# Sparse attention and a feed-forward block on one core: token blocks of 512 instead of 256, with the split done in place and the weights converted without GpSimd

## The chip, the cores and the metric

The kernel runs on one core of a Trainium2 chip. The metric is the device time of one execution in microseconds (us). The kernel before took 999.59 us, the median of three runs (999.54 to 1001.24).

Engines go by the profile's names: PE is TensorE's products and PEld its weight loads, DVE is VectorE, ACT ScalarE, POOL GpSimd, SP SyncE. An engine works through its own list of instructions in order; the engines meet at semaphores. DMA transfers are issued from the lists of SP and ACT.

## What is computed

Eight batches, eight heads, 576 positions, head size 64. Heads 0 to 3 attend within 32 positions back (local), heads 4 to 7 to earlier positions of the same class modulo 32 (strided). The result, 576 x 512 per batch, goes through a low-rank mix over the positions and a feed-forward layer:

```
scores = scale * q @ k.T                              # masked, then softmax
x      = softmax(scores) @ v                          # all heads side by side: (8, 576, 512)
u      = x + ((x.T @ U) @ V).T                        # U: 576 x 32, V: 32 x 576
out    = u + relu(u @ w_ch1) @ w_ch2                  # w_ch1: 512 x 2048, w_ch2: 2048 x 512
```

U, V and both weights arrive as 64-bit floats; q, k and v are 32-bit. For the large products each operand is split into a high and a low part (`uh`, `ul`; `gh`, `gl`; two parts of each weight chunk), and three products (high-high, high-low, low-high) are summed.

## The kernel before, in words

**Feed-forward part.** Tokens are cut into tiles of 128. A batch has four tiles of its own and half a tile more; the halves of two batches share the tile `xt`. Two tiles make a block of 256 tokens, so there are 18 blocks. A block runs 16 steps, one per chunk of 128 hidden units. `gemm1` (L546) makes 12 products of 256 columns into `ph`; ScalarE's relu makes `gh` (L550), VectorE `gl` (L551). `gemm2` (L562) makes six products of 512 columns per step into `acc`, two steps behind `gemm1`. `finish` (L569) adds `acc` to `u` and stores it.

**Ahead of a block.** `transposes` brings `u` into columns by token. For the first three blocks TensorE does it (L512) and ScalarE and VectorE split the result (L516, L517). For the others VectorE transposes 32 x 32 pieces (`bt`, L525), 16 transfers on SP move them into `u`, and L534 and L535 split them into new buffers `uh`, `ul`, five buffers of tag `u` in turn.

**Weights.** `weights` turns 64-bit words into 32-bit floats with one ScalarE instruction (L115) and three of VectorE (L117, L118, L120), in halves of 512 columns; ScalarE casts the high part (L162), GpSimd subtracts for the low part (L163). Sixteen chunks of 1 MB are loaded, three at first (`AHEAD`) and then each after the GpSimd copy L144 that waits for a converted chunk. Four chunks are converted ahead of the first product (`PRE`), and the first two blocks run interleaved (`NLEAD`, `SKEW`) while the rest are converted.

**Attention.** Two heads make a pair. A pair has mask and scores (L234, L240), softmax (L249, L250, L254), transposes (L261, L264), outputs (L273) and a normalisation (L283 to L285). Batches 0 and 1 do all heads so; their two strided pairs are computed in class order, and their outputs `od` go through DRAM to come back in token order into `xg`. Batches 2 to 7 do the local pairs so, and the strided heads on GpSimd and VectorE: products on GpSimd (L327, L355), each summed by a VectorE reduction (L329, L357), the result copied into `xg` by ScalarE (L372, L376). `mix_t` (L393, L397) makes `x.T @ U` as four products side by side in the array, whose parts are added (L402, L404) and split into `tst` (L407 to L409); `mix_u` (L419, L421, L427, L428) adds the correction to `x`.

**What sets the order.** A loop over the steps interleaves `gemm1`, `gemm2`, conversion and attention by windows of steps (`W0`, `W1`, `N_LOCAL`, `CONVM`). A scheduler then reorders each engine's instructions by its own estimate of the times. PSUM holds one `acc` of two banks, two `ph` and two `px` of two banks each; attention and mixing use `px`, and `acc` too until the first product.

Of the kernel before, what the change touches and what calls it, by code (L numbers as in the profile page):

```python
# [16 lines left out]
ATT_BUFS = 4  # L17
NSP = 2
N_STEPS_1 = 90
N_LOCAL = 48  # L20
# [3 lines left out]
W0, W1 = 2, 29  # L24
N_PE_T = 3
AHEAD = 3
PRE = 4
CONVM = 1.35
NLEAD = 2
SKEW = 2  # L30
CLA = 2
S_END = 16
# [5 lines left out]
def fused_kernel(ctx, tc, pairs, strided, U, V, w_in, masks, eye, out):  # L38
# [7 lines left out]
    NDC = DM // 128  # L46

# [33 lines left out]
    def psx2():  # L81

        banks["n"] += 1
        if banks["prefix"] and banks["n"] % 3 == 0:
            return ps_acc.tile([128, 2, 512], F32, name="acc")
        return ps_x.tile([128, 2, 512], F32, name="px")
# [8 lines left out]

    def od_dma(out, in_):
        nc.scalar.dma_start(out=out, in_=in_)
# [3 lines left out]
    mask_s = ubuf([128, 320], "mask_s", BF16)  # L101
    mask_l, ident_b = masks_sb[:, 0:320], masks_sb[:, 320:448]
    U_sb = const.tile([128, 5, R], F32, name="U_sb")
    Vst = const.tile([96, S], F32R, name="Vst")
    raws, w_parts = {}, {}
# [32 lines left out]

    def load_weights():
        for fc in range(NFC):  # L140
            raw = raws[fc] = const.tile([128, 1024], I64, name=f"w{fc}", tag=f"w{fc}")
            if fc >= AHEAD:
                done = w_parts[fc - AHEAD].bitcast(F32)
                nc.gpsimd.tensor_copy(out=raw.bitcast(F32)[:, 0:1], in_=done[:, 1, 1, 0:1])  # L144
            nc.sync.dma_start(out=raw, in_=w_in[128 * fc:128 * fc + 128, :])
            yield

    def weights():
        for fc in range(NFC):
            load_ahead(fc + 1)  # L150
            fs = []
            for i in range(2):
                early = i and fc < NFC - AHEAD - 2
                cv = late_part[fc % 2][:, 1536:2048] if early else ap_.tile([128, 512], F32, name="cv", tag="cv", bufs=2)
                behind = [marks[k][2] for k in ("less", "exp")] if fc < PRE else marks["split0"]
                with tc.issue_after(behind[0]), tc.issue_after(behind[1]):
                    fs.append(to_f32(raws[fc][:, 512 * i:512 * i + 512], cv, 128, 512))
                if not i:
                    yield
            parts = w_parts[fc] = const.tile([128, 2, 2, 512], F32R, name=f"w{fc}", tag=f"w{fc}")  # L160
            for i in range(2):
                nc.scalar.copy(out=parts[:, i, 0], in_=fs[i])  # L162
                nc.gpsimd.tensor_tensor(out=parts[:, i, 1], in0=fs[i], in1=parts[:, i, 0].bitcast(F32), op=ALU.subtract)  # L163
            load_ahead(fc + 1 + AHEAD)
            yield

    late_part = []
# [110 lines left out]
    def normalised(op, main, last, p0):  # L278

        rt = ap_.tile([128, 16], F32, name="rt", tag="mx", bufs=3)[:, 0:10].rearrange("p (h t) -> p h t", h=2)  # L280
        for o, r, dst in ((op[:, :, 0:4], rt[:, :, 0:4], main.rearrange("p t (h d) -> p h t d", h=2)),
# [3 lines left out]
            nc.vector.tensor_tensor(out=dst, in0=o[..., 0:D], in1=r.broadcast_to(list(r.shape) + [D]), op=ALU.mult)  # L285

    def local_pairs(b):
# [3 lines left out]
        for pr in range(2):  # L291
            kT, qT, vt = load_pair(b, pr)
            for _ in range(3):
# [438 lines left out]
```

## Time and profile before

| | |
|---|---|
| profiled execution | 999.63 us |
| its span, first to last instruction | 997.7 us |
| PE, PEld busy | 940.9, 812.8 us |
| DVE, ACT, POOL busy | 594.0, 265.3, 360.2 us |
| granted TensorE clock, mean | 0.997 |
| first product of the feed-forward part (L546) | at 69.8 us |
| products of L546; L562 | 3,456 of 256 columns; 1,728 of 512 columns |
| weight conversion on GpSimd (L163) | 32 x 1.36 to 1.59 us |
| moved by DMA | 72.72 MB |

In a row of the timeline or of the chain the first number is the start in us, the second the length. A row of a group gives the count, busy time in all, mean of one in ns, and the idle time of the engine before it with what ended that. Products are pipelined: their mean length (288 ns at L546) is longer than the distance between them. In a row of the windows stand the stretch, its length, and for each engine the busy time and the number of instructions; after them the granted clock, the DMA share and GB/s.

### The profile page before, as it was taken

Reading aid. Unit: us, or ns where it says so; the run is one execution under the profiler, and the core shown is the slowest. Engines: PE = TensorE matmul, PEld = TensorE weight load, DVE = VectorE, ACT = ScalarE, POOL = GpSimd, SP = SyncE. Lnnn points to the kernel's source line nnn. Section 1 sums busy time; section 2 is a strip of 40 time slices with the busy share of each in tenths; the row PEclk is TensorE's granted clock in tenths of the full one; section 3 lists DMA queues with packets and bytes.
Section 4 is the critical chain, followed back from the end, with each engine's and each line's share of the span. In section 5 each row is a group of like instructions: output and inputs, shape, how many; then the busy total and the mean of one; then the engine's idle time right before and its main releaser. Section 6 shows DMA issues by size and latency. Waiting matters only on the chain.

```text
span 997.7 us, 20318 instructions
## 1 busy us (share of the span) xinstructions
PE 940.9 (94%) x8524; PEld 812.8 (81%) x8524; DVE 594.0 (60%) x1102; ACT 265.3 (27%) x617; POOL 360.2 (36%) x379
## 2 busy tenths in 40 slices
PE   4257999999999999999999999999999999999997
PEld 3236878888888898888888888888888889999996
DVE  4849876886856577215686568746874744212121
ACT  3325442143113411113411242124211421111110
POOL 0405537645733376003394238604761400000000
PEclk9999999999999999999999999999999999999999
DMA  9725750212111221102121121113211000101000
GB/s 362 281 59 203 242 175 2 86 51 101 41 60 53 62 73 40 33 15 76 49 77 46 36 96 70 46 43 96 71 46 43 2 22 22 43 1 43 1 22 22
DMA packets 38731, 72.72 MB, mean 73 GB/s; under 512 B 5968, under 2 KB 25296, under 8 KB 35824
## 3 DMA queue, kind: packets, MB, share of 16 engines
q1 hardware_dynamic: 34864, 69.07, 20.7%
q10 hardware_dynamic: 3776, 2.36, 0.9%
q8 instruction: 67, 1.10, 0.5%
q14 instruction: 24, 0.20, 0.1%
HBM read 52.92 MB, written 10.62 MB: 64 GB/s over the span
## 4 chain that ended last, share of the span: by engine, by line
PE 85%; DVE 8%; DMA 3%; issue 2%; ACT 1%; ACTq 0%; POOL 0%; SPq 0%; DVEq 0%
PE ph L546 40%; PE acc L562 37%; PE px L240 2%; DVE cv L120 1%; DVE cv L118 1%; PE px L562 1%; PE px L273 1%; DMA xg<-in_V_dram 1%; PE px L393 1%; PE px L419 1%; PE px L261 1%; DVE spare L118 1%; DMA od<-ring 1%; DVE cv L117 1%; DVE spare L117 1%
## 5 line engine op out<-in xcount | busy, mean ns | idle before, releaser
L546 PE MATMUL ph<-uh,w 128*128 128x256 f32 x2304 | 474.7, 288 | 7.3 <-DVE gl L551 7.2
L546 PEld LDWEIGHTS ph<-uh,w 128*128 128x128 f32 x2304 | 378.6, 190 | 24.9 <-DVE gl L551 9.7
L562 PE MATMUL acc<-w,gh 128*128 128x512 f32 x1088 | 341.8, 394 | 0.0
L546 PE MATMUL ph<-ul,w 128*128 128x256 f32 x1152 | 330.8, 287 | 0.2 <-DVE ul L517 0.2
L551 DVE SCALAR_TENSOR_TENSOR gl<-ph,gh 128x256 fp32r<-128x256 f32 x288 | 121.4, 422 | 276.1 <-ACT gh L550 274.9
L355 POOL TENSOR_TENSOR tmp<-st,s_st 128x448 f32<-128x448 f32 (+7 forms) x162 | 139.1, 878 | 310.0 <-DVE st L357 240.4
L550 ACT ACTIVATE gh<-ph 128x256 fp32r<-128x256 f32 x288 | 110.4, 383 | 517.4 <-PE ph L546 473.7
L546 PEld LDWEIGHTS ph<-ul,w 128*128 128x128 f32 x1152 | 217.3, 189 | 9.4 <-DVE ul L517 0.4
L562 PEld LDWEIGHTS acc<-w,gh 128*128 128x128 f32 x1088 | 193.6, 188 | 29.6
L562 PE MATMUL acc<-w,gl 128*128 128x512 f32 x544 | 214.2, 394 | 0.0
L327 POOL TENSOR_TENSOR tmp<-st 128x576 f32<-128x576 f32 (+6 forms) x162 | 168.5, 1072 | 27.5 <-DVE s_st L329 21.1
L357 DVE TENSOR_REDUCE st<-tmp 128x64 f32<-128x64 f32 (+8 forms) x162 | 137.4, 875 | 8.1 <-POOL tmp L355 7.4
L562 PEld LDWEIGHTS acc<-w,gl 128*128 128x128 f32 x544 | 102.2, 188 | 19.1
L329 DVE TENSOR_REDUCE s_st<-tmp 128x9 f32<-128x576 f32 (+6 forms) x162 | 89.0, 566 | 12.1 <-POOL tmp L327 11.4
L163 POOL TENSOR_TENSOR w<-cv,w 128x512 fp32r<-128x512 f32 x21 | 28.4, 1364 | 99.0 <-ACT w L162 94.6
L372 ACT COPY xg<-st 32x256 f32<-32x256 f32 x96 | 38.7, 404 | 21.1 <-DVE st L357 19.7
L240 PEld LDWEIGHTS px<-qkv 64*32 64x32 f32 x1368 | 20.3, 112 | 20.6 <-issue 17.4
L240 PE MATMUL px<-qkv 64*32 64x64 f32 (+1 forms) x1368 | 31.8, 237 | 0.6 <-issue 0.6
L404 DVE TENSOR_TENSOR ta<-px,ta 32x256 f32<-32x256 f32 x42 | 17.6, 420 | 22.5 <-ACT ta L402 21.4
L535 DVE TENSOR_TENSOR ul<-u,uh 128x1024 fp32r<-128x1024 f32 x15 | 19.6, 1304 | 16.9 <-ACT uh L534 16.9
L421 DVE TENSOR_TENSOR xg<-px,xg 128x512 f32<-128x512 f32 x30 | 19.5, 682 | 8.7 <-PE px L419 8.7
L569 DVE TENSOR_TENSOR xg<-acc,xg 128x512 f32<-128x512 f32 x30 | 19.5, 685 | 7.5 <-PE acc L562 7.4
(106 smaller groups left out, 545.1 us busy)
## 6 DMA issues: line engine op xcount, KB each, us to landing
w<-in_w_dram SPq DMA_DIRECT2D x16, 1024.0 KB, 5.2
qkv<-in_pairs_dram SPq DMA_DIRECT2D x19, 585.0 KB, 5.8
qkv<-in_pairs_dram SPq DMA_DIRECT2D x19, 576.0 KB, 4.3
out_dram<-xg SPq DMA_DIRECT2D x32, 256.0 KB, 2.1
u<-bt SPq DMA_DIRECT2D x240, 32.0 KB, 1.9
st<-in_strided_dram SPq DMA_DIRECT2D x6, 1152.0 KB, 5.5
st<-in_strided_dram SPq DMA_DIRECT2D x6, 576.0 KB, 3.9
xg<-od ACTq DMA_DIRECT2D x8, 128.0 KB, 4.9
```

Of the source, the lines that this page charges most:

```text
L117: nc.vector.tensor_scalar(out=i, in0=i, scalar1=3, scalar2=None, op0=ALU.logical_shift_left)
L163: nc.gpsimd.tensor_tensor(out=parts[:, i, 1], in0=fs[i], in1=parts[:, i, 0].bitcast(F32), op=ALU.subtract)
L240: nc.tensor.matmul(sp[32 * c4:32 * c4 + 32, hh, x0:64 * t + 64], qT[rows, 32 * c:32 * c + 32], kT[rows, k0:32 * c + 32], start=False, stop ...
L327: nc.gpsimd.tensor_tensor(out=tmp[:, 0:n], in0=sk[:, j0:j0 + n], in1=sq[:, i:i + 1].broadcast_to([128, n, D]), op=ALU.mult)
L329: late.append(lambda tmp=tmp, n=n, i=i, j0=j0: nc.vector.tensor_reduce(out=s_st[:, i, j0:j0 + n], in_=tmp[:, 0:n], axis=AX.X, op=ALU.add))
L355: nc.gpsimd.tensor_tensor(out=tv, in0=sv[:, 0:i + 1, d0:d0 + step], in1=s_st[:, i, 0:i + 1].broadcast_to([128, i + 1, step]), op=ALU.mult)
L357: late.append(lambda tv=tv, i=i, d0=d0, step=step: nc.vector.tensor_reduce(out=o_st[:, i, d0:d0 + step], in_=tv.rearrange("p j d -> p d j" ...
L372: nc.scalar.copy(out=xg[32 * i4:32 * i4 + 32, :, cs], in_=o_st[rows, i4:16:4, :])
L546: nc.tensor.matmul(ph[:, 0:W], w_parts[fc][:, 0, part, 128 * dc:128 * dc + 128], ut[:, :, :, dc, :], start=(dc == 0 and i == 0), stop=(dc ...
L550: nc.scalar.activation(out=gh[:, 0:W], in_=ph[:, 0:W], func=AF.Relu)
L551: nc.vector.scalar_tensor_tensor(out=gl[:, 0:W], in0=ph[:, 0:W], scalar=0.0, in1=gh[:, 0:W].bitcast(F32), op0=ALU.max, op1=ALU.subtract)
L562: nc.tensor.matmul(accs[n][:, s, :], gt[:, cs], w_parts[fc][:, 1, part, :], start=(fc == 0 and i == 0), stop=(fc == NFC - 1 and i == 2))
```

## The change

- A block is one batch's 512 tokens (`gemm1`, L565: 12 products of 512 columns per step; `gemm2`, L579: 12 per step into two `acc` tiles, four banks). The half tiles of all batches make a ninth block: `mix_u` of every second batch stores `xt` to DRAM (`ud`), and `tail_block` reads four of them back. So there are 9 blocks of 16 steps. `gemm2` runs one step behind `gemm1`.
- There is one `uh`, one `ul` and one untransposed-order buffer `raw`. `split` (L556, L557) overwrites `uh` and `ul` after the block's last `gemm1`. The block of batch 0 is split straight out of PSUM (L526, L527), that of batch 1 goes from PSUM to `raw` (L521); the others go by `bt` (L536) and 32 transfers, half issued by SP and half by ScalarE (L105).
- Weights are converted in whole chunks of 1,024 columns; the subtraction (L174) is VectorE's. Two chunks are converted ahead of the first product. Two chunks are loaded at first; the third waits, by a GpSimd copy (L155), for `tst` of batch 0, and the further loads and batch 1's follow it on SP.
- The strided heads start only when all weights are converted.
- `mix_t` of batches 0 and 1 makes its five products one after another in the same columns (L410, L412) and needs no additions.
- `px` has one buffer of two banks instead of two. Before the first product two of three uses take `acc` instead of one of three. Other buffers: `att` five instead of four, `half` three, `wide` one (for the strided operands and for the conversion).

The core of the diff:

```diff
-NLEAD = 2
-SKEW = 2
-PRE = 4
+PRE = 2
+FREE = 2
-    ps_acc = ctx.enter_context(tc.tile_pool(name="ps_acc", bufs=1, space=bass.MemoryType.PSUM))
+    ps_acc = ctx.enter_context(tc.tile_pool(name="ps_acc", bufs=2, space=bass.MemoryType.PSUM))
-    ps_x = ctx.enter_context(tc.tile_pool(name="ps_x", bufs=2, space=bass.MemoryType.PSUM))
+    ps_x = ctx.enter_context(tc.tile_pool(name="ps_x", bufs=1, space=bass.MemoryType.PSUM))
...
+            if fc == FREE:
+                nc.gpsimd.tensor_copy(out=words_in.bitcast(F32)[0:32, 0:1], in_=tsts[0].bitcast(F32)[0:32, 256:257])
+            if fc > FREE:
+                with tc.issue_after(loads["gate"]):
+                    nc.sync.dma_start(out=words_in, in_=w_in[128 * fc:128 * fc + 128, :])
...
-            for i in range(2):
-                nc.scalar.copy(out=parts[:, i, 0], in_=fs[i])
-                nc.gpsimd.tensor_tensor(out=parts[:, i, 1], in0=fs[i], in1=parts[:, i, 0].bitcast(F32), op=ALU.subtract)
+            nc.scalar.copy(out=parts[:, :, 0], in_=fv)
+            nc.vector.tensor_tensor(out=parts[:, :, 1], in0=fv, in1=parts[:, :, 0].bitcast(F32), op=ALU.subtract)
...
+        if b < NSP:
+            for j in range(4):
+                nc.tensor.matmul(ps_a[0:32, :], U_sb[:, j, :], xg[:, j, cs], start=j == 0, stop=False,
+                                 skip_group_check=True, tile_position=(0, 0))
...
+            for a in range(4):
+                for q in range(4):
+                    (od_dma if q % 2 else dma)(out=raw[32 * q:32 * q + 32, t:t + 2, a].rearrange("p s d x -> p s (d x)"),
+                                               in_=bt[32 * a:32 * a + 32, q].rearrange("p s d x -> p s (d x)"))
...
+    def split(n):
+        for dc in range(NDC):
+            hi, lo = (u[:, dc, :].rearrange("p (s a x) -> p s a x", s=4, a=4) for u in (uh, ul))
+            nc.scalar.copy(out=hi, in_=raw[:, :, :, dc, :])
+            nc.vector.tensor_tensor(out=lo, in0=raw[:, :, :, dc, :], in1=hi.bitcast(F32), op=ALU.subtract)
...
-        gh = mp.tile([128, 256], F32R, name="gh", bufs=3)
+        gh = mp.tile([128, 512], F32R, name="gh", bufs=2)
...
+    for step, (n, fc) in enumerate(steps):
+        if n == 0:
+            convert(2 * fc + 2)
+        pend.append((n, fc) + gemm1(fc))
+        if fc == NFC - 1 and n + 1 < NB:
+            split(n + 1)
+        if n == 0:
+            convert(2 * (fc + CLA) + 2)
+        advance(2 * step)
+        if len(pend) > 1:
+            item = pend.pop(0)
+            gemm2(*item)
+            if item[1] == NFC - 1:
+                finish(item[0])
+        advance(2 * step + 1)
```

The scheduler's order changes with it. In the kernel before, TensorE's list has batch 1's last outputs (L273) and its mix (L393, L397) inside the steps of the first two blocks; two pieces of that list:

```order
L562 MATMUL px<-w_819,gh 128x512 x2
L273 MATMUL px<-qkv,PT 32x65 x36
L562 MATMUL px<-w_819,gl 128x512
...
L546 MATMUL ph<-uh,w_1474 128x256
L393 MATMUL px<-xg,U_sb 32x256 x4
L397 MATMUL px<-xt,U_sb 32x64 x4
L546 MATMUL ph<-uh,w_1474 128x256
```

In the new list the same work of batch 1 (L287 is its last outputs, L410 and L412 the mix, L443 and L450 the correction, L518 the transposes) stands here, after the last product of block 0 (`w_1548` is the sixteenth chunk) and ahead of the first of block 1 (`w_468` is the first chunk):

```order
L579 MATMUL acc<-w_1548,gl 128x512
L287 MATMUL px<-v,PT 32x65 x36
L410 MATMUL px<-xg,U_sb 32x256 x4
L412 MATMUL px<-xt,U_sb 32x256
L410 MATMUL px<-xg,U_sb 32x256 x4
L412 MATMUL px<-xt,U_sb 32x256
L443 MATMUL px<-tst,Vst 128x512 x2
L518 MATMUL px<-ident,xg 128x128 x8
L443 MATMUL px<-tst,Vst 128x512 x2
L518 MATMUL px<-ident,xg 128x128 x8
L450 MATMUL px<-tst,Vst 128x512
L565 MATMUL ph<-uh,w_468 128x512
```

The chain of outputs, mix, correction and transposes has moved out of the steps to the boundary of two blocks. The second place is VectorE's list where batch 3's strided scores are summed. In the kernel before, a piece of it reads (L551 makes `gl`, L329 sums a GpSimd product):

```order
L551 SCALAR_TENSOR_TENSOR gl<-ph,gh 128x256
L329 TENSOR_REDUCE s_st<-tmp 128x9
L329 TENSOR_REDUCE s_st<-tmp 128x6
L421 TENSOR_TENSOR xg<-px,xg 128x512
L551 SCALAR_TENSOR_TENSOR gl<-ph,gh 128x256
L421 TENSOR_TENSOR xg<-px,xg 128x512
L329 TENSOR_REDUCE s_st<-tmp 128x9
L329 TENSOR_REDUCE s_st<-tmp 128x7
L428 TENSOR_TENSOR xt<-px,xt 64x512
L329 TENSOR_REDUCE s_st<-tmp 128x9
L551 SCALAR_TENSOR_TENSOR gl<-ph,gh 128x256
```

In the new list L570 makes `gl` and L342 is the reduction; this is the end of the stretch in block 1 between the `gl` of step 13 and those of steps 14 and 15:

```order
L342 TENSOR_REDUCE s_st<-tmp 128x9
L342 TENSOR_REDUCE s_st<-tmp 128x6
L342 TENSOR_REDUCE s_st<-tmp 128x9
L342 TENSOR_REDUCE s_st<-tmp 128x7
L342 TENSOR_REDUCE s_st<-tmp 128x9
L342 TENSOR_REDUCE s_st<-tmp 128x8
L342 TENSOR_REDUCE s_st<-tmp 128x9 x2
L351 TENSOR_REDUCE m_st<-s_st 128x18
L352 TENSOR_TENSOR s_st<-s_st,m_st 128x324
L570 SCALAR_TENSOR_TENSOR gl<-ph,gh 128x512 x2
```

Where two or three reductions stood between one `gl` and the next, 18 stand in this stretch. The third place is ScalarE's list beside it. Before, it has only relu and split there (L550 makes `gh`, L534 the split), since SP issues the transfers:

```order
L550 ACTIVATE gh<-ph 128x256 x6
L340 ACTIVATE s_st<-s_st 128x324
L550 ACTIVATE gh<-ph 128x256
L534 CAST uh<-u 128x1024
L550 ACTIVATE gh<-ph 128x256 x9
```

Now, in block 1 (L569 makes `gh`, L105 issues the transfers of `bt`, L556 is the split):

```order
L569 ACTIVATE gh<-ph 128x512 x2
L105 DMA raw<-bt 32x2x128 x16
L569 ACTIVATE gh<-ph 128x512 x2
L353 ACTIVATE s_st<-s_st 128x324
L556 CAST uh<-raw 128x512 x4
L569 ACTIVATE gh<-ph 128x512 x2
```

Sixteen transfers now stand on ScalarE between the `gh` of steps 13 and 14; in the later blocks they come in pieces of at most eight with a `gh` between them.

More of the change, by code (lines that the diff above doesn't have):

```diff
@@ L94, in dma, with later_dma @@
         nc.sync.dma_start(out=out, in_=in_)
+    def later_dma(out, in_):
+        if "gate" in loads and len(raws) > FREE:
+            with tc.issue_after(loads["gate"]):
+                dma(out, in_)
+        else:
+            dma(out, in_)
     def od_dma(out, in_):
@@ L146, in load_weights @@
             yield
     def weights():
+        cvs = wide_buffer("cv")
         for fc in range(NFC):
             load_ahead(fc + 1)
-            fs = []
-            for i in range(2):
[L153 to L159, printed above, removed]
+            behind = (marks["norm"][1], marks["exp"][3]) if fc < PRE else marks["split0"]
+            with tc.issue_after(behind[0]), tc.issue_after(behind[1]):
+                f = to_f32(raws[fc], cvs[:, 1152 * (fc % 2):1152 * (fc % 2) + 1024], 128, 1024)
+            fv = f.rearrange("p (i x) -> p i x", i=2)
+            yield
@@ L422, in mix_u @@
                 yield
-            if b == 0 and t < 2 * NLEAD:
-                yield from transposes(t // 2)
-                marks.setdefault("split0", marks["split"])
+            if b < NSP:
+                yield from transposes_pe(b, t)
         pv = psx1()
@@ L450, in first_attention @@
         pairs0 = early_pairs(b, ORDER0)
-        spare = [const.tile([128, 2048], F32, name="ring", tag=f"w{fc}") for fc in (NFC - 3, NFC - 4)]
-        ring.extend(s[:, 640 * k:640 * k + 640] for k in range(3) for s in spare)
         next(pairs0[0])
@@ L456, in first_attention @@
         dma(out=ident, in_=eye)
-        next(pairs0[1])
-        next(pairs0[2])
         sw = small_weights()
         next(sw)
-        next(pairs0[3])
+        for pair in pairs0[1:]:
+            next(pair)
         yield
@@ L464, in first_attention @@
             if len(marks.get("less", ())) >= 2:
-                with tc.issue_after(marks["less"][1]):
-                    next(sw, None)
+                next(sw, None)
             yield
@@ new lines, in strided_end, with advance @@
+    def strided_end(b):
+        nonlocal sgen, sb
+        if sb == b:
+            for _ in sgen:
+                pass
+            sgen = None
+            sb += 1
+    gen, done = None, 0
+    def advance(slot):
+        nonlocal gen, done
+        n, k = divmod(slot, 2 * NFC)
+        if k == 0 and n < B:
+            gen, done = (attention(n + 1) if n + 1 < B else tail_block()), 0
+        if gen is not None:
+            a0, a1, total = A_EARLY if n == 0 else A_LATE if n + 1 < B else A_TAIL
+            want = 10 ** 6 if k >= a1 else total * (k + 1 - a0) // (a1 - a0)
```

282 lines of the change are left out of this document (122 added, 160 removed).

## The prediction

> **What bounds the kernel now.** I read the page first: shares of the span, the 40 slices, the chain that ended last.
>
> ```profile
> span 997.7 us, 20318 instructions
> PE 940.9 (94%) x8524; PEld 812.8 (81%) x8524; DVE 594.0 (60%) x1102; ACT 265.3 (27%) x617; POOL 360.2 (36%) x379
> PE   4257999999999999999999999999999999999997
> PE 85%; DVE 8%; DMA 3%; issue 2%; ACT 1%; ACTq 0%; POOL 0%; SPq 0%; DVEq 0%
> ```
>
> TensorE is full from about 125 us on and carries 85% of the chain. So two things count: how much work TensorE has, and how long the start lasts. Next the chain in order of time, at the start and in the last 100 us, where only the feed-forward part runs.
>
> ```profile
> 38.96 6.59 DMA od<-ring
> 45.54 4.64 issue
> 51.53 5.02 DMA xg<-od
> 56.65 1.93 PE ph L393 x16
> ...
> 904.83 2.90 PE ph L546 x24
> 907.74 3.17 PE acc L562 x14
> 949.85 2.91 PE ph L546 x24
> 987.87 4.09 PE acc L562 x18
> ```
>
> Twenty-four 256-wide products take 2.90 us, 121 ns each; fourteen 512-wide ones take 3.17 us, 226 ns each. One block of 16 steps lasts from 904.83 to 949.85, 45.02 us, so 18 blocks are 810.4 us of the span. The last product ends at 992.0, which leaves 5.7 us for the last addition and the store. At the start the chain is the round trip of `od` through DRAM, from 39 to 56.7 us. The timeline shows where the feed-forward part begins:
>
> ```profile
> 63.50 1.19 PE L419 MATMUL px<-tst,Vst 96*128 96x512 f32 x2 [4.34 <-DVE tst L409]
> 69.79 0.50 PE L546 MATMUL ph<-uh,w 128*128 128x256 f32 x2
> ```
>
> From 69.8 us to the end are 927.9 us. Without the blocks' 810.4, 117.5 us are left for attention on TensorE, waits and the tail.
>
> **Wider products.** A step now has 12 products of 512 columns at L565 where two steps had 24 of 256. At 226 ns, a step of 24 wide products is 5.436 us and 144 steps are 782.8 us: **27.6 us less**. The rate is that of L562, whose weights also change with every product. [...]
>
> **The start.** Two weight chunks, not four, are converted ahead, and VectorE finishes the two by-class pairs first.
>
> ```profile
> 22.00:38.90 16.90, 5.03 (x6) 1.00 0.71 264
> 22.00:38.90 16.90, 5.55 (x6) 1.00 0.71 264
> 22.00:38.90 16.90, 3.55 (x6) 1.00 0.71 264
> 29.85 1.75 DVE L120 SCALAR_TENSOR_TENSOR spare<-w,spare 128x512 int32<-128x512 int32 x1
> 35.75 0.67 DVE L120 SCALAR_TENSOR_TENSOR cv<-w,cv 128x512 int32<-128x512 int32 x1
> 36.35 0.68 DVE L118 SCALAR_TENSOR_TENSOR spare<-w,spare 128x512 int32<-128x512 int32 x1
> 41.24 0.41 DVE L117 TENSOR_SCALAR spare<-spare 128x512 int32<-128x512 int32 x1
> 115.23 2.24 ACTq L97 DMA_DIRECT2D od<-o_sb  x2
> 122.73 1.80 ACTq L97 DMA_DIRECT2D xg<-od  x4
> ```
>
> The first three rows are VectorE's conversion lines L118, L120 and L117 between 22.0 and 38.9 us: 14.1 of 16.9 us, ahead of the second pair's `od`. With them behind it, that store moves from 39 to about 28 us. Its way back was 11.2 us to the read (38.96 to 50.18) among weight loads; batch 1's, in less traffic, took 7.5 (the last two rows), and the new order has no load in flight there, since the third weight waits for `tst`. I take 6 to 7 us. Then follow 6.5 us to the landing, the serial mix (below) and the correction, now of four tiles ahead of the first product where two were enough: 7.2 us instead of 6.3. The first product starts at **56 us**. Bounds: 66 if the conversions were not what held the pair, 50 if the outputs of the last pair overlap the landing.
>
> **The first block.** TensorE needs 87 us for 16 steps, and batch 1's four pairs go between them. These rows, from the timeline of a later batch, price attention on TensorE: transposes, outputs, mask, scores, mix, correction, and a split-off piece of scores.
>
> ```profile
> 463.02 0.80 PE L261 MATMUL px<-ident,s_sb 128*128 128x128 f32 x5
> 467.71 0.97 PE L273 MATMUL px<-qkv,PT 64*32 64x65 f32 x72
> 472.75 0.45 PE L234 MATMUL px<-masks_sb 128*128 128x320 bf16 x2
> 473.12 0.92 PE L240 MATMUL px<-qkv 64*32 64x32 f32 x72
> 490.17 0.64 PE L393 MATMUL px<-xg,U_sb 128*32 128x256 f32 x8
> 490.74 0.32 PE L397 MATMUL px<-xt,U_sb 64*32 64x64 f32 x8
> 513.78 0.63 PE L419 MATMUL px<-tst,Vst 96*128 96x512 f32 x2
> 553.46 0.30 PE L240 MATMUL px<-qkv 64*32 64x64 f32 x2
> ```
>
> A pair is 0.80 + 0.97 + 0.45 + 0.92 = 3.14 us; four pairs without the last outputs are 11.6. VectorE now does all of a chunk's conversion. No GpSimd instruction runs beside it, so I take 0.68 us for 512 columns and not the 1.75 that L120 took beside GpSimd: about 0.6 + 3 x 1.15 us for 1,024 columns, and 0.7 for `gl`, 4.8 us a step, some 6.5 with batch 1's softmax. TensorE's step with attention is 6.1. VectorE may be late by 4.5 us (`gl` is ready 1.4 us after its product and needed a step later), so I add **3 us** (0 to 12, were the operations half again as long).
>
> **The first block change.** In the new order batch 1's last outputs, its mix, correction, transposes and split all stand behind the last product of block 0 and ahead of block 1, with nothing between. With one buffer of `px`, each waits for the reader of the one before.
>
> ```profile
> L285 DVE TENSOR_TENSOR xg<-px,rt 128x512 f32<-128x512 f32 x15 | 10.3, 686 | 0.3
> L407 ACT CAST tst<-ta 32x256 fp32r<-32x256 f32 x16 | 6.5, 404 | 11.5 <-DVE ta L404 11.2
> L409 DVE TENSOR_TENSOR tst<-ta,tst 32x256 fp32r<-32x256 f32 x16 | 11.8, 737 | 1.4 <-ACT tst L407 0.9
> L421 DVE TENSOR_TENSOR xg<-px,xg 128x512 f32<-128x512 f32 x30 | 19.5, 682 | 8.7 <-PE px L419 8.7
> L516 ACT CAST uh<-px 128x512 fp32r<-128x512 f32 x6 | 3.5, 585 | 5.7 <-PE px L512 5.6
> ```
>
> Outputs 0.97; normalise 1.9 (0.69 and five smaller ones); two mixes of five serial products, about 0.32 each if four side by side take one's time (0.08 to 0.43), 1.6, and 1.2 for `tst`: 5.6; twice a correction 0.63, two additions 1.3, eight transposes 1.3 (five take 0.80) and two copies 1.2: 8.8; the first split 0.6. That is 17.9, about 2 for fourteen hand-overs, and 4 for strided reductions between them on VectorE: **24 us** (12 to 35).
>
> **Block 1.** Its VectorE order has 18 strided reductions between the `gl` of step 13 and of step 14, each behind a GpSimd product, and ScalarE issues 16 transfers between the same two `gh`.
>
> ```profile
> L327 POOL TENSOR_TENSOR tmp<-st 128x576 f32<-128x576 f32 x66 | 94.6, 1442 | 9.0 <-DVE s_st L329 8.8
> 519.26 10.77 SPq L94 DMA_DIRECT2D u<-bt  x16
> ```
>
> GpSimd needs 21 us for those 18 (eleven at 1.44), TensorE's step 6, the slack is 4.5, and a product or two runs ahead: **9 us** lost (0 to 15). Sixteen issues at 0.67 us are 10.8 us on ScalarE at the same place, hidden behind the 21; without these they would cost about half. In blocks 2 to 6 reductions and issues stand between more `gh`, never more than 9.6 us of GpSimd or eight issues (5.4 us) in a row, within the slack: nothing.
>
> **The other changes.** `split` waits for the block's last readers; the two pending L579 groups (5.4 us) cover it. VectorE then has four `ul`, six reductions and four additions of `finish` (0.68 each) before the next `gl`, about 11 us against 9.7 + 0.5 until it is needed: 1.3 us at each of six, **8 us** (0 to 25 if `finish` holds `acc`).
>
> **Attention of six batches.** Two pairs 6.3, two mixes 1.9, correction 1.1, about 2 for thirteen switches: 11.3 us each, **68** in all (60 to 88; now it is split into more pieces, as the 0.30 us for two products shows).
>
> **Sum.** 56 + 782.8 + 11.6 + 3 + 24 + 9 + 68 + 8 + 5.7 = 968.1 us of span. The profiled execution took 999.63 us for 997.7, so 1.9 go on top: **970.0 us**. It stands 0.04 us from the median of the three runs, 999.59.
>
> **Rivals.** (a) The ends meet on the other side: blocks 2 to 6 lose as block 1 does, because eight issues on ScalarE wait for VectorE's transposes, which queue behind GpSimd's products, and the `gh` behind them comes a step late. At 10 us in each of five blocks the time is 1020. It decides from 5.9 us a block on (29.6 / 5). Against it stands the order with a `gh` between the groups; for it, that GpSimd is the slowest engine there: 9%. (b) The start is not shorter, because the `od` trip and the four-tile correction set it anyway: 984; the unexplained 4.64 us of issue speak for it: 13%. (c) The first change costs 12 us, since the mix overlaps the normalise, and VectorE keeps up: 955, 15%. [...] What is forecast has 60%.
>
> **Numbers.** Range 952 to 994: it takes in (b), (c), (d) and the unknowns' bounds around the sum, and leaves out (a) and about a tenth at the ends. A measurement here tells about 0.2%, 2 us, from no change (the runs span 999.54 to 1001.24). Faster 0.88; within it 0.03, from (d); slower 0.09, from (a).
>
> **What would show it.** Wide products 226 ns apart; the first one at 50 to 60 us; a gap of about 20 us on TensorE at the end of the first block and one of about 9 in the second, behind `gl`; then no gap over 3 us. [...]

## The result, and the profile after

The changed kernel takes 965.04 us (median of 4 runs, 964.16 to 966.90), the kernel before took 999.57 us beside it. The ratio is 0.9655, 95% interval 0.9636 to 0.9673: faster by 3.4%. The prediction said 970.0 us, 952 to 994, faster with a chance of 0.88. The profiled execution took 964.96 us for a span of 963.2.

The page after the change:

```profile
span 963.2 us, 16256 instructions
PE 907.2 (94%) x6780; PEld 717.3 (74%) x6780; DVE 561.2 (58%) x927; ACT 240.5 (25%) x456; POOL 305.2 (32%) x335
PE   4699996799959999999999999999999999999996
PEclk9799998799979999999999999999999999999999
PE 87%; DVE 5%; POOL 2%; DMA 2%; ACT 1%; issue 1%; SPq 0%; ACTq 0%; DVEq 0%; POOLq 0%
```

A slice is 24 us. TensorE is full from the third slice on (48 us), before the change from the fifth (100 us). Two dents follow that the old row did not have: slices 7 and 8 (144 to 192 us), the boundary of blocks 0 and 1, and slice 12 (264 to 289 us), the end of block 1. After that the row is nines to the tail. So the answer lies in four places: start, first boundary, end of block 1, tail.

**The start**, from the timeline (a row: start, length, engine, line, what it is, and in brackets the idle time before it with what ended it):

```profile
26.81 1.05 ACTq L105 DMA_DIRECT2D od<-late  x2
29.47 2.81 ACTq L105 DMA_DIRECT2D xg<-od  x4
34.50 3.59 PE L410 MATMUL ph<-xg,U_sb 128*32 128x256 f32 x8 [3.05 <-DMA xg<-od]
51.40 0.73 PE L565 MATMUL ph<-uh,w 128*128 128x512 f32 x2 [0.67 <-ACT uh L526]
```

The second pair's `od` leaves in two stores, the first at 26.8 us (before: at 38.4; the 38.96 of the prediction is the second one). It is read back at 29.5 and used at 34.5: 7.7 us from the first store to the mix, where it was 18.3. Most of what went is the landing of the two stores, after which the read is issued: they took 2.4 and 1.9 us to land, before the change 11.6 and 11.2. The first product comes at 51.4 us, 18.4 us earlier than before.

**The first boundary** on TensorE:

```profile
152.18 0.97 PE L287 MATMUL px<-v,PT 64*32 64x65 f32 x72
158.78 3.59 PE L410 MATMUL px<-xg,U_sb 128*32 128x256 f32 x8 [5.63 <-DMA qk<-in_pairs_dram]
164.57 1.91 PE L410 MATMUL px<-xg,U_sb 128*32 128x256 f32 x8 [1.27 <-DVE tst L433]
168.30 0.73 PE L443 MATMUL px<-tst,Vst 96*128 96x512 f32 x2 [1.27 <-DVE tst L433]
174.00 1.22 PE L443 MATMUL px<-tst,Vst 96*128 96x512 f32 x2 [0.67 <-ACT raw L521]
180.83 1.22 PE L565 MATMUL ph<-uh,w 128*128 128x512 f32 x2
```

From batch 1's last outputs to block 1's first product are 28.7 us. The bracket at 158.78 names a transfer, but the instruction ahead of it in time is VectorE's last normalisation (L299, 158.39 to 158.68), which frees `px`: a releaser by the profile is the last event and not always the cause. Two pairs of rows do the same work in different times: L410 takes 3.59 and 1.91 us, L443 1.22 and 0.73. The windows show why (columns as before; the third number from the end is the granted clock):

```profile
158.78:163.30 4.52, 4.52 (x10) 1.41 (x10) 2.77 (x6) 0.00 (x0) 4.52 (x5) 0.52 0.11 42
163.30:166.50 3.20, 1.93 (x10) 0.88 (x10) 2.15 (x4) 0.72 (x2) 3.20 (x5) 1.00 0.00 0
172.20:176.60 4.40, 2.34 (x6) 1.22 (x7) 1.29 (x2) 0.58 (x1) 1.39 (x2) 0.50 0.00 0
```

After the 5.63 us of idling the granted clock is 0.52 up to 163.30 us and 1.00 from there to 166.50; from 172.20 to 176.60 us, where TensorE is busy 2.34 of 4.40 us, it is 0.50.

**The end of block 1**, all engines:

```profile
270.16 11.40 ACTq L105 DMA_DIRECT2D raw<-bt  x16
270.84 16.33 POOL L340 TENSOR_TENSOR tmp<-st 128x576 f32<-128x576 f32 x14 [0.23 <-DVE s_st L342]
278.38 0.43 PE L248 MATMUL px<-masks_sb 128*128 128x320 bf16 x2 [3.54 <-DVE xt L451]
281.65 1.08 ACT L569 ACTIVATE gh<-ph 128x512 fp32r<-128x512 f32 x2 [17.74 <-DVE s_st L342]
282.30 2.07 PE L579 MATMUL acc<-w,gh 128*128 128x512 f32 x4 [3.49 <-ACT gh L569]
288.93 1.28 DVE L570 SCALAR_TENSOR_TENSOR gl<-ph,gh 128x512 fp32r<-128x512 f32 x2
289.67 0.79 PE L579 MATMUL acc<-w,gl 128*128 128x512 f32 x1 [5.29 <-DVE gl L570]
```

TensorE idles 3.54 + 3.49 + 5.29 = 12.3 us. The first wait is for `px`, which VectorE's L451 frees between its reductions. It seems to cost nothing by itself, since the products behind it need `gh`, which stands behind ScalarE's sixteen issues (270.16 to 281.56) and comes only then; TensorE goes on at 282.3 us. After that it waits for `gl`, which stands behind VectorE's reductions, and these behind GpSimd's products (to 287.2).

**The tail.** VectorE's additions of `finish` mark the ends of blocks 6 and 8; SP's list holds the last stores:

```profile
780.58 2.48 DVE L585 TENSOR_TENSOR xg<-acc,xg 128x512 f32<-128x512 f32 x4 [0.81 <-PE acc L579]
954.66 2.48 DVE L585 TENSOR_TENSOR xg<-acc,xg 128x512 f32<-128x512 f32 x4 [3.21 <-PE acc L579]
955.38 5.03 SPq L95 DMA_DIRECT2D out_dram<-xg  x8
```

Blocks 7 and 8 hold nothing but products: 174.08 us for 32 steps, 5.44 us a step. The last product ends at 955.5; eight stores of 0.63 us each, one behind the other, make the tail 7.7 us.

### The profile page after: what moved, and what is told of

It reads as the page before. It is cut to its first block, busy times and chain, and to the rows that moved or that the text cites. A ratio compares the mean times of both kernels' runs of the same rounds, so it can differ in the third digit from the quotient of the medians.

```text
span 963.2 us, 16256 instructions
## 1 busy us (share of the span) xinstructions
PE 907.2 (94%) x6780; PEld 717.3 (74%) x6780; DVE 561.2 (58%) x927; ACT 240.5 (25%) x456; POOL 305.2 (32%) x335
## 4 chain that ended last, share of the span: by engine, by line
PE 87%; DVE 5%; POOL 2%; DMA 2%; ACT 1%; issue 1%; SPq 0%; ACTq 0%; DVEq 0%; POOLq 0%
PE acc L579 39%; PE ph L565 39%; POOL tmp L340 2%; PE px L287 2%; PE px L254 1%; PE px L275 1%; DVE st L370 1%; PE px L443 1%; PE px L418 1%; DVE xg L445 1%; PE px L410 1%; PE ph L410 1%; DMA st<-in_strided_dram 1%; DMA xg<-in_V_dram 1%; DMA qk<-in_pairs_dram 0%
## 5 line engine op out<-in xcount | busy, mean ns | idle before, releaser
L565 PE MATMUL ph<-uh,w 128*128 128x512 f32 x1152 | 382.8, 393 | 0.7 <-ACT uh L526 0.7
L579 PE MATMUL acc<-w,gh 128*128 128x512 f32 x1152 | 358.6, 395 | 3.5 <-ACT gh L569 3.5
L579 PEld LDWEIGHTS acc<-w,gh 128*128 128x128 f32 x1152 | 216.0, 189 | 50.3 <-ACT gh L569 3.8
L565 PEld LDWEIGHTS ph<-uh,w 128*128 128x128 f32 x1152 | 216.3, 188 | 47.4 <-ACT uh L526 1.0
L570 DVE SCALAR_TENSOR_TENSOR gl<-ph,gh 128x512 fp32r<-128x512 f32 x144 | 98.9, 688 | 252.6 <-ACT gh L569 252.2
L579 PE MATMUL acc<-w,gl 128*128 128x512 f32 x576 | 220.3, 394 | 6.2 <-DVE gl L570 6.2
L565 PE MATMUL ph<-ul,w 128*128 128x512 f32 x576 | 225.4, 391 | 0.0
L569 ACT ACTIVATE gh<-ph 128x512 fp32r<-128x512 f32 x144 | 85.8, 596 | 469.7 <-PE ph L565 381.2
L579 PEld LDWEIGHTS acc<-w,gl 128*128 128x128 f32 x576 | 108.7, 189 | 30.5 <-DVE gl L570 7.3
L565 PEld LDWEIGHTS ph<-ul,w 128*128 128x128 f32 x576 | 108.5, 188 | 22.9 <-DVE ul L527 0.4
L342 DVE TENSOR_REDUCE s_st<-tmp 128x9 f32<-128x576 f32 (+6 forms) x162 | 87.7, 564 | 29.1 <-POOL tmp L340 28.3
L329 POOL MEMSET s_st<- 128x324 f32 x6 | 2.2, 368 | 96.6 <-PE px L275 88.3
L557 DVE TENSOR_TENSOR ul<-raw,uh 128x512 fp32r<-128x512 f32 x32 | 20.8, 677 | 7.0 <-ACT uh L556 7.0
L125 ACT ACTIVATE cv<-w 128x1024 f32<-128x1024 f32 x16 | 18.2, 1153 | 16.6 <-DVE w L174 16.5
```

What stands on the lines that cost most here:

```text
L342: late.append(lambda tmp=tmp, n=n, i=i, j0=j0: nc.vector.tensor_reduce(out=s_st[:, i, j0:j0 + n], in_=tmp[:, 0:n], axis=AX.X, op=ALU.add))
L557: nc.vector.tensor_tensor(out=lo, in0=raw[:, :, :, dc, :], in1=hi.bitcast(F32), op=ALU.subtract)
L565: nc.tensor.matmul(ph, w_parts[fc][:, 0, part, 128 * dc:128 * dc + 128], ut[:, dc, :], start=(dc == 0 and i == 0), stop=(dc == NDC - 1 and ...
L569: nc.scalar.activation(out=gh, in_=ph, func=AF.Relu)
L570: nc.vector.scalar_tensor_tensor(out=gl, in0=ph, scalar=0.0, in1=gh.bitcast(F32), op0=ALU.max, op1=ALU.subtract)
L579: nc.tensor.matmul(accs[n][s // 2][:, s % 2, :], gt[:, cs], w_parts[fc][:, 1, part, :], start=(fc == 0 and i == 0), stop=(fc == NFC - 1 an ...
```

## The experiments

Each is the changed kernel with the edit shown, so it is compared with 965.04 us; ratios are against the kernel before on the same chip, which took 998.5 to 999.4 us there. "Trip" is the time from the first store of the pair's `od` to the first mix product. Lines left out of an edit are marked by three dots.

**Wide products.** `gemm1` in blocks 7 and 8 in halves of 256 columns:

```diff
...
+        w = 256 if n >= B - 1 else 512
+        for dc, cols in [(dc, slice(c, c + w)) for c in range(0, 512, w) for dc in range(NDC)]:
-                nc.tensor.matmul(ph, w_parts[fc][:, 0, part, 128 * dc:128 * dc + 128], ut[:, dc, :],
+                nc.tensor.matmul(ph[:, cols], w_parts[fc][:, 0, part, 128 * dc:128 * dc + 128], ut[:, dc, cols],
...
```

> Only in blocks 7 and 8 (the last batch's own tokens and the half tiles) gemm1's 512-column products are cut into two of 256 columns, each with its own weight load; all else is unchanged. Theory of the prediction: two narrow products cost 242 ns, a wide one 226 ns, so 32 steps of 12 lose 16 ns each, 6.1 us in all: 971 us, and a step of block 8 lasts 5.63 us instead of 5.44. [...]

970.72 us, ratio 0.9717 (0.9701 to 0.9733): 5.7 us more. TensorE's timeline in block 8 (L566 is `gemm1`, L580 `gemm2`), the first products of two steps:

```profile
902.10 0.28 PE L566 MATMUL ph<-uh,w 128*128 128x256 f32 x1
...
907.72 0.28 PE L566 MATMUL ph<-uh,w 128*128 128x256 f32 x1
```

A step is 5.62 us instead of 5.44. The theory holds: from the end of block 6 to that of block 8 are 5.74 us more, so over the 384 products two halves cost 15 ns more than a whole (16 were expected). The length of the old kernel's steps is back with it (45.02 us for 16 half steps, 5.63 for two). So the gain is shown for two of nine blocks; for the others it follows from the same product distances, and in all it is 810.4 less 783.4, 27.0 us, for the 27.6 of the prediction.

**Conversions first.** The two chunks converted ahead are not held behind the second pair:

```diff
-            behind = (marks["norm"][1], marks["exp"][3]) if fc < PRE else marks["split0"]
+            behind = None if fc < PRE else marks["split0"]
...
-        if len(marks.get("exp", ())) >= 4 and len(marks.get("norm", ())) >= 2:
+        if len(marks.get("exp", ())) >= 1:
```

> The two chunks converted ahead of the first product are no longer held behind the second by-class pair, so VectorE's list has their eight instructions (8.7 us) ahead of that pair's normalisation. Theory of the prediction: the conversions set when the pair's outputs are stored, so that store is issued 6 to 9 us later than at 26.8 us, the first product of the feed-forward part comes at 57 to 60 us instead of 51.4, and the time is 971 to 974 us. Rival: the start is set by the trip through DRAM and the correction whatever VectorE does first; first product at 51 to 53 us, time 965 to 967 us.

972.61 us, ratio 0.9734 (0.9716 to 0.9751). The store of `od` moves to 33.5 us, the first product to 57.7:

```profile
33.47 1.05 ACTq L105 DMA_DIRECT2D od<-late  x2
40.62 3.59 PE L412 MATMUL ph<-xg,U_sb 128*32 128x256 f32 x8 [5.09 <-DMA xg<-od]
57.66 1.22 PE L567 MATMUL ph<-uh,w 128*128 128x512 f32 x2 [0.68 <-ACT uh L528]
```

The trip is 7.2 us, no longer than without the edit. The theory holds: where the conversions stand sets the store, 6.7 us later, and the store sets the first product, 6.3 us later.

**Loads during the trip**, five and seven free chunks for two:

```diff
-FREE = 2
+FREE = 5
```

> Five weight chunks are loaded at first instead of two, so 3 MB more are in flight while od makes its trip through DRAM; the order on VectorE ahead of the first product stays. Theory of the prediction: load traffic slows the trip; from the store's issue to the first mix product it takes 11 to 15 us instead of 7.7, the first product comes at 55 to 59 us, time 969 to 972 us. Rival: the trip costs what it costs whatever else is moved: first product at 51 to 52 us, time within 1.5 us of 965.

969.23 us, ratio 0.9699 (0.9681 to 0.9716). Store at 27.08, mix at 37.02: the trip is 9.9 us and the first product at 54.5, between the two theories. The loads were over by about 32 us, before `od` was read back. So with seven:

> As with five free chunks, but seven: 5 MB more than in the changed kernel are in flight, at some 350 to 400 GB/s until about 38 us, so through nearly all of the trip of od. Theory: the trip is as long as the load traffic around it; from the store's issue at 27 us to the first mix product it takes 12 to 16 us (7.7 with two free chunks, 9.9 with five), the first product comes at 57 to 61 us. Rival: the 2.2 us that five chunks cost are all there is; trip 9 to 11 us, first product at 53 to 55 us.

974.56 us, ratio 0.9748 (0.9731 to 0.9766). This kernel's timeline:

```profile
28.33 0.37 ACTq L105 DMA_DIRECT2D od<-late  x1
44.21 6.22 PE L410 MATMUL ph<-xg,U_sb 128*32 128x256 f32 x16 [9.71 <-DMA xg<-od]
61.31 0.73 PE L565 MATMUL ph<-uh,w 128*128 128x512 f32 x2 [0.33 <-ACT uh L526]
```

And the trip in the windows (last number: GB/s moved in it), of the changed kernel, of this one, and of the kernel before, there from the pair's second store on:

```profile
26.81:34.50 7.69, 2.32 (x78) 1.74 (x79) 7.01 (x12) 3.44 (x5) 0.00 (x0) 0.71 0.43 117
```

```profile
28.33:44.21 15.88, 4.04 (x149) 3.14 (x150) 10.73 (x20) 4.02 (x5) 0.00 (x0) 0.50 0.77 290
```

```profile
38.96:56.65 17.69, 2.74 (x78) 2.04 (x79) 6.76 (x18) 2.93 (x6) 5.00 (x6) 1.00 0.87 294
```

The trip is 7.7 us at 117 GB/s, 9.9 with five free chunks at 203, 15.9 here at 290, and was 18.3 before the change at 294. What grows is the landing of the two stores: 2.4 and 1.9 us, then 5.4 and 5.0, here 11.5 and 9.0, and before the change 11.6 and 11.2. Here the second store was also issued late, at 30.98 us, though VectorE had finished its data at 27.1. Counted from the end of VectorE's last normalisation of the pair instead, the mix comes after 7.2, 9.4, 17.1 and, before the change, 17.7 us: seven free chunks bring the old trip back almost whole. The theory holds, with a first product 0.3 us behind its range. Holding the loads back until `tst` is worth up to 10 us at the start.

**The old start put together**, three edits: conversions first, `PRE = 4`, `FREE = 5`.

> The start of the kernel before is put together again in the new kernel: four chunks are converted ahead of the first product, not held behind the second by-class pair, and five weight chunks are loaded at first. Theory: the shorter start comes from these alone (conversions ahead of the pair's outputs, and load traffic during their trip), so od is stored at 39 to 42 us, the trip takes 10 us or more, and the first product comes at 66 to 70 us as before the change; 978 to 984 us. Rival: a good part of the gain has another source (other PSUM buffers, the serial mix); the first product comes at 63 us or earlier, 975 us or less.

970.32 us, ratio 0.9718 (0.9701 to 0.9735).

```profile
39.94 1.05 ACTq L105 DMA_DIRECT2D od<-late  x2
47.08 3.59 PE L412 MATMUL ph<-xg,U_sb 128*32 128x256 f32 x8 [2.99 <-DMA xg<-od]
62.90 0.74 PE L567 MATMUL ph<-uh,w 128*128 128x512 f32 x2 [0.32 <-ACT uh L528]
```

By the signs set ahead the rival came true: the first product before 63 us, the time below 975. The store was right (39.9, before the change 38.4); the trip was not: 7.1 us, since the five loads are over by then (124 GB/s during the trip), while 294 GB/s were moved in the kernel before. So the conversions are 11.5 of the 18.4 us. The other 6.9 are the trip's 11.1 (18.3 less 7.1), less the later store (1.5), the serial mix (8.2 us from mix to correction for 6.9) and the correction (7.6 for 6.3). That load traffic makes this trip long is shown by the run with seven free chunks (15.9 us at 290 GB/s), not by this one.

The time rose by 5.3 us only, not by 11.5: the first boundary came back shorter. From the first product to block 1's first are 122.3 us here and 129.4 in the changed kernel. With two chunks fewer to convert inside block 0, batch 1's last outputs came 95.4 us after the first product instead of 100.8, still beside products; their normalisation was covered, the first mix ran in 1.91 us, and the boundary lasted 21.5 us. This fits a VectorE whose conversions set how late that attention runs; the run changes the start as well, so it is no proof.

**Subtraction back on GpSimd**:

```diff
-            nc.vector.tensor_tensor(out=parts[:, :, 1], in0=fv, in1=parts[:, :, 0].bitcast(F32), op=ALU.subtract)
+            nc.gpsimd.tensor_tensor(out=parts[:, :, 1], in0=fv, in1=parts[:, :, 0].bitcast(F32), op=ALU.subtract)
```

> The subtraction of the weight conversion goes back to GpSimd; whole chunks, order of blocks and products stay. The scheduler answers with other places for batch 1's last outputs and first mix (inside block 0), so the lengths of block 0 and of its boundary are compared, not the time alone. Theory of the prediction: beside a GpSimd subtraction VectorE's 1,024-column instructions grow from 1.22 us to 2 us or more, so VectorE gains little from the 1.22 us it gives up per chunk and block 0 (100.8 us from its first product to its last now, attention of batch 1 included) is 0 to 10 us longer. Rival: VectorE is relieved, its instructions keep their 1.22 us and block 0 is not longer.

972.25 us, ratio 0.9732 (0.9715 to 0.9748). The groups of the conversion in block 0 (count, busy time, mean ns), the changed kernel first:

```profile
L128 DVE SCALAR_TENSOR_TENSOR cv<-w,cv 128x1024 int32<-128x1024 int32 x14 | 17.1, 1220 | 0.1
L130 DVE SCALAR_TENSOR_TENSOR cv<-w,cv 128x1024 int32<-128x1024 int32 x14 | 17.0, 1218 | 0.0
L127 DVE TENSOR_SCALAR cv<-cv 128x1024 int32<-128x1024 int32 x14 | 9.6, 687 | 0.5 <-ACT cv L125 0.3
```

```profile
L174 POOL TENSOR_TENSOR w<-cv,w 128x1024 fp32r<-128x1024 f32 x14 | 38.2, 2735 | 57.6 <-ACT w L173 50.6 <-DMA w<-in_w_dram 4.8 <-DMA v<-in_pairs_dram 2.3
L130 DVE SCALAR_TENSOR_TENSOR cv<-w,cv 128x1024 int32<-128x1024 int32 x14 | 24.3, 1732 | 0.1
L128 DVE SCALAR_TENSOR_TENSOR cv<-w,cv 128x1024 int32<-128x1024 int32 x14 | 23.3, 1661 | 0.3
L127 DVE TENSOR_SCALAR cv<-cv 128x1024 int32<-128x1024 int32 x14 | 15.1, 1077 | 5.2 <-ACT cv L125 5.0
L570 DVE SCALAR_TENSOR_TENSOR gl<-ph,gh 128x512 fp32r<-128x512 f32 x15 | 10.2, 681 | 10.6 <-ACT gh L569 10.6
```

VectorE gives up 1.22 us a chunk and pays 0.51 + 0.44 + 0.39 = 1.34 back. From first product to block 1's first are 136.2 us, 6.8 more, nearly the whole difference. Block 0 alone takes 115.2 us for 100.8, which is more than the 10 us longer that were expected: TensorE idles 9.4 us in it. Its boundary is shorter, 21.0 us for 28.7, since the last outputs fall inside the block. `gl`, whose first operand is in PSUM, kept its time (681 ns against 686).

The two means hide how it happens. An L128 or L130 that starts while a subtraction runs ends 1.1 us after the subtraction's end and so lasts 2.7 to 3.4 us; these are seven of the 28, and the others keep their 1.2 us. Beside the subtraction from 108.71 to 111.89 us, for example, L130 lasts 2.82 us (from 110.16) and `gl` 0.68 (from 109.55). So the theory holds for the instructions that meet a subtraction: they look as if they waited for its end.

**The stall of block 1.** Three edits: batch 2's strided heads finished two steps earlier, batch 3's started six steps later, and all transfers of the transposes on SP:

```diff
-S1 = (20, 14)
+S1 = (16, 14)
```

> Batch 2's strided heads are to be finished four slots (two steps) earlier in block 1, so that its mix and transposes come earlier: ScalarE's 16 issues then stand as 8 and 8 with a gh between, and at most 7 reductions stand ahead of the last gl instead of 19. Theory: block 1's 12.3 us of idle TensorE (and some 2 us of products at a low clock behind it) come from that collision alone and go; 951 to 954 us. Rival: the collision only names the waits, and the stall comes back because the split of block 2 needs the transposes, which GpSimd's pace sets; 960 us or more.

956.87 us, ratio 0.9573 (0.9559 to 0.9587). In block 1 TensorE idles 3.02 + 1.47 us instead of 12.3. The gain, 8.2 us, is less than was expected, and the time lies between the theory's and the rival's: 3 us of waiting for the correction stayed, and the first boundary was 1.7 us longer, since here the second mix too took 3.62 us, as the first does in the changed kernel at a granted clock of 0.52 (3.59).

```diff
-S0 = {b: 32 * (b - 1) - 12 for b in range(2, 8)}
+S0 = {b: 32 * (b - 1) - (12 if b != 3 else 0) for b in range(2, 8)}
```

> Batch 3's strided heads start 12 slots (six steps) later, with block 2. In block 1 only 4 reductions are left ahead of the last gl, and ScalarE's 16 issues stay where they are; in block 2 now 15 reductions and 16 issues meet. Theory (reductions behind GpSimd set the later half of the stall, the issues the first half): block 1 idles 7 us instead of 12.3, block 2 idles about 12 where it had none; 970 to 974 us. Rival (the issues cost nothing by themselves): block 1 idles under 2 us. Other rival (the reductions cost nothing by themselves): block 1 still idles 12 us.

972.74 us, ratio 0.9734 (0.9720 to 0.9749). TensorE in block 1 and in block 2:

```profile
278.18 0.43 PE L248 MATMUL px<-masks_sb 128*128 128x320 bf16 x2 [0.77 <-DVE xt L451]
284.00 2.07 PE L579 MATMUL acc<-w,gh 128*128 128x512 f32 x4 [5.39 <-ACT gh L569]
...
388.28 1.49 PE L579 MATMUL acc<-w,gh 128*128 128x512 f32 x4 [2.19 <-ACT gh L569]
395.42 0.80 PE L579 MATMUL acc<-w,gl 128*128 128x512 f32 x1 [5.65 <-DVE gl L570]
```

Block 1 idles 6.2 us with the issues alone, 5.4 of it for `gh`; block 2, where 15 reductions and 16 issues now meet, idles 9.3 us with the same waits (1.4 of it for `px`, ahead of the rows shown). Neither cause is free by itself: both rivals fall.

```diff
-                    (od_dma if q % 2 else dma)(out=raw[...], in_=bt[...])
+                    dma(out=raw[...], in_=bt[...])
```

> All 32 transfers of a batch's transposes are issued by SP, none by ScalarE. The list then has 6 and 4 reductions ahead of the last two gl of block 1. Theory: neither gh nor gl is held in block 1, but 32 issues of 0.73 us one behind the other take 23 us, so raw is complete at about 295 us, and block 2's first product, which needs the split of raw, comes at about 296 us as it does now (294): the stall moves from gl to the split, 963 to 972 us. Rival (ScalarE's issues and the reductions were the whole cause): block 2 starts 10 us or more earlier, 951 to 955 us.

973.02 us, ratio 0.9745 (0.9712 to 0.9778). SP and TensorE:

```profile
268.46 21.48 SPq L95 DMA_DIRECT2D raw<-bt  x32
292.16 1.22 PE L565 MATMUL ph<-uh,w 128*128 128x512 f32 x2 [12.48 <-ACT uh L556]
```

The stall only changed its name: 32 issues one behind the other take 21.5 us, the split waits for the last, and TensorE idles 12.5 us for `uh` (block 1 to block 2: 114.1 us; in the changed kernel 113.2). The time is 1 us above the theory's range, and its four runs are far apart, 971.2 to 978.8 us.

**The first boundary.** One edit gives batch 1's mix a buffer of `ph`:

```diff
-        ps_a = psx1()[:, 0:256]
+        ps_a = (ps_h.tile([128, 512], F32, name="ph") if b < NSP else psx1())[:, 0:256]
```

> The mix of batch 1 uses a buffer of gemm1's ph instead of the one px buffer. The scheduler's list then has the outputs of the last pair, the mix and half of the correction of batch 1 inside the last steps of block 0. Theory: of the 28.7 us between block 0's last product and block 1's first one some 10 us are TensorE's own work at full clock and the rest are waits between engines and work at a low clock; beside products the waits are hidden, so 12 to 18 us are saved: 947 to 953 us. Rival: gemm1 needs the same ph buffers, so products wait inside block 0 for batch 1's outputs on their trip through DRAM, and what is won at the boundary is lost there: 962 to 970 us.

969.99 us, ratio 0.9706 (0.9690 to 0.9723). The rival holds. Waits stand inside block 0 now; the longest:

```profile
134.35 3.59 PE L410 MATMUL ph<-xg,U_sb 128*32 128x256 f32 x8 [7.61 <-DMA xg<-od]
```

The products behind it wait for batch 1's trip through DRAM. Block 1 starts at 186.5 us instead of 180.8. The next edit leaves the buffers alone and changes the pace and the place of one mix:

```diff
-CLA = 2
-A_EARLY = (1, 28, N_EARLY)
+CLA = 0
+A_EARLY = (1, 20, N_EARLY)
...
-            yield from run_staggered(early_pairs(b, ORDER1), LAGB)
+            yield from run_staggered(early_pairs(b, ORDER1) + [mix_t(b, 1)], LAGB)
             yield "free"
-            yield from mix_t(b, 1)
```

> Three numbers of the order only: chunks are converted no further ahead than needed (CLA 0 for 2), batch 1's attention is spread over 20 slots of block 0 instead of 28, and the mix of its by-class columns is put beside the last pair. The list then has the first mix and the last pair's outputs inside block 0; only the second mix, the correction and the transposes stay at the boundary. Theory: VectorE, full with conversions up to 123 us, is what pushed batch 1's attention to the end of block 0; so the boundary falls from 28.7 to 19 to 22 us and block 0 grows by the 2.5 us of the mix: 957 to 961 us. Rival: conversions that come just in time hold the products in block 0, which loses what the boundary wins: 963 us or more.

959.38 us, ratio 0.9609 (0.9595 to 0.9623). Three rows of TensorE there (L287 is batch 1's last outputs, L450 the last work ahead of block 1's first product):

```profile
149.94 0.98 PE L287 MATMUL px<-v,PT 64*32 64x65 f32 x72
...
155.63 1.89 PE L410 MATMUL px<-xg,U_sb 128*32 128x256 f32 x8 [1.76 <-DVE xt L299]
...
171.47 0.79 PE L450 MATMUL px<-tst,Vst 96*128 96x512 f32 x1 [0.68 <-ACT raw L520]
```

The boundary lasts 18.2 us (153.9 to 172.1) and block 0 is 2.6 us longer, about as forecast. The reason given in the theory is not shown: VectorE's last conversion ends at 122.6 us here and at 123.0 in the changed kernel, and batch 1's last outputs come 99.4 us after the first product, hardly sooner than before (100.8). From first product to block 1's first are 7.8 us less. Of these, 5.8 are the first mix, which has left the chain (in the changed kernel it takes the time from 158.78 to 164.57); 1.4 are the earlier outputs, and 0.7 the rest. The wait ahead of the remaining mix is 1.8 us, and that mix took 1.89 us, as the second does in the changed kernel at a granted clock of 1.00 (1.91). What conversions inside the block can cost is seen better in the old start put together, where two fewer brought the outputs 5.4 us forward.

**All three together**, with the tail's stores on two queues: the edit above, `S1 = (12, 14)`, and

```diff
-                    dma(out=out[2 * s + bb, 512:576, :], in_=ot[64 * bb:64 * bb + 64, :])
+                    (od_dma if bb else dma)(out=out[2 * s + bb, 512:576, :], in_=ot[64 * bb:64 * bb + 64, :])
```

> The order of the run before, batch 2's strided heads finished eight slots earlier (S1 12 for 20), and the eight stores of the last block issued half by SP, half by ScalarE. Theory: the three costs at the boundary, in block 1 and in the tail are separate, so their gains add up: about 5.5 us, 8 to 12 us and 2.3 us, 946 to 950 us. Rival: the tail is set by the landing of the last store and not by eight issues of 0.63 us, and what goes from block 1 comes back at block 2's split: 954 us or more.

941.55 us (940.27 to 942.75), ratio 0.9430 (0.9414 to 0.9446): 2.4% under the changed kernel, the fastest here. From block 1's first product to its first addition of `finish` are 101.6 us (172.9 to 274.5); with the same start but the old `S1` they were 117.5. In block 2 nothing came back (97.2 us for 100.2). So the stall was worth 15.9 us there, its idle time and the slow products behind it (granted clock 0.50 from 282.3 to 292.0 us in the changed kernel), more than the 8 to 12 that were expected, and the time is below the 946 to 950 us of the theory. `S1 = (12, 14)` was not run alone. The tail, from the last product's end (933.2) to the end of the span (939.6), is 6.4 us instead of 7.7: less than the 2.3 us hoped for.

## Why the prediction was right, step by step

| term of the sum | predicted | measured |
|---|---|---|
| first product | 56 | 51.4 |
| 144 steps | 782.8 | 783.4 (5.44 each, from blocks 7 and 8) |
| batch 1 in block 0, VectorE late | 11.6 + 3 | 13.7 |
| first block change | 24 | 28.7 |
| block 1's stall | 9 | about 14 |
| attention of six batches, six block changes | 68 + 8 | about 64 |
| tail | 5.7 | 7.7 |
| span | 968.1 | 963.2 |

The stall is the difference of block 1 with and without it (in the changed kernel and in the last run, counted from L450 to the last additions of `finish`, 13 to 14 us); the attention is what is left of the blocks 1 to 6, so the column adds up by the way it is made.

- **Wide products**: right to 0.1%, and shown by itself. No run shows a saving as small as the one that (d) brings into the range and the 0.03; the runs show 5.74 us lost by halving the 384 products of blocks 7 and 8, 15 ns each.
- **The start**: the mechanism was right; rival (b) falls. The step that was off is the way back: 6 to 7 us to the read, taken from batch 1's trip in the old kernel, and 6.5 from there to the mix, taken from batch 0's; measured 2.7 and 5.0. The trip went with its traffic in these runs (7.7 us at 117 GB/s, 9.9 at 203, 15.9 at 290), and batch 1's old one was in more of it (228 GB/s between 115 and 123 us) than was thought; the new one runs at 117. The 4.64 us of issue that the prediction calls unexplained are the end of the old stores' landing, 11.2 us from 38.96. Against this, from mix to correction took 9.9 us where the sum leaves 7.8: the first half of the mix ran at a granted clock of 0.50 (3.59 us for 1.91).
- **VectorE in block 0**: TensorE waited once for `gl`, 0.9 us. But that VectorE was full until 123 us seems to have cost: with two chunks fewer to convert in the block batch 1's last outputs came 5.4 us earlier and the boundary was 7.2 us shorter. The prediction took the boundary from the list and did not see why the list was so. Rival (c), 12 us at the boundary, falls.
- **The first change**: 28.7 for 24 us, inside 12 to 35. What lacked is the low clock: the first mix took 3.59 us at 0.52 where the second took 1.91 at 1.00, and the correction and transposes from 172.2 us on ran at 0.50. The strided reductions were there, as said.
- **Block 1's stall**: place and causes right, size too small. It idled 12.3 us, and about 2 more, by the lengths of the rows, went to products at a granted clock of 0.50 behind it (282.3 to 292.0 us). "Hidden behind" fits the trace, where `gh` is made from 281.7 us on and `gl` only from 288.9; with four reductions left the issues cost 6.2 us, half of the stall, as was said.
- **Other block changes and attention**: 12 us too dear. No idle time of TensorE stands in the blocks 2 to 8, so the 8 us were nothing, and attention costs 10.7 us a batch and not 11.3. Rival (a) falls as well.
- **The tail**: taken from the old kernel's end; in the new one eight stores of 0.63 us stand behind the last additions, and spreading them over two queues took 1.3 us off.
- **A misreading**: the old kernel's row of slices has TensorE full from the fifth slice, 100 us, not from 125. No term rests on it.

So three terms that were too small (about 12 us in all) met two that were too large (17 us), and the total came closer than its parts. That the span is off by only 4.9 us is in part luck.

## What to carry to other kernels

Where a scheduler leaves a chain of small dependent steps at a boundary, look for a step that can go ahead: here one mix put beside the last pair took 5.8 us out of the chain, while giving the chain another buffer only moved the wait. Ask also which engine was full ahead of the chain: with two weight chunks fewer to convert there it started 5.4 us sooner. A stall at which two engines hold back the operands of one step is removed by moving the work that collides, not by moving it to another queue. A round trip through DRAM should be priced with the traffic that will be around it (here 7.7 us at 117 GB/s and 15.9 at 290), and idle TensorE with the low clock seen behind it (here 0.52 after 5.63 us, by which a mix took 3.59 us for 1.91).

## What was not expected of the hardware

- The profile's clock record missed a slow stretch here. The old kernel's page has 1.00 throughout its start, but its own row at 63.50 us takes 1.19 us for the two products that take 0.63 at 513.78 us: about half clock, estimated from the two lengths. Of 33 other executions of the old kernel, at 997.4 to 1000.4 us, all but one have a mean clock of 0.966 to 0.972. So the mean clocks of the two profiles, 0.997 before and 0.971 after, do not show that the new kernel is throttled more. Lengths of like instructions were the safer sign.
- The trip of `od` through DRAM took 7.1 to 18.3 us from store to use in these runs, with 117 to 294 GB/s moved during it, and most of the difference is the landing of the stores (1.9 to 11.6 us).
- In the run with the subtraction on GpSimd, VectorE's instruction with one input (L127) also grew, from 687 to 1,077 ns in the mean; the four that met a subtraction lasted 1.72 to 2.85 us. `gl`, with an operand in PSUM, did not grow (681 ns, 686 without it).
